# A two-layer Fourier-mixing and expert kernel on one core: row maxima by one reduction, buffers and order changed around them

## The chip, the cores and the metric

The kernel runs on one core of a Trainium2 chip, as one launch that takes the whole input and gives the whole output. The time is device microseconds of that core; the figure for the kernel is the median of its runs. The core has five engines that the text speaks of: TensorE (PE in the profile; its weight loads are listed as PEld), VectorE (DVE), ScalarE (ACT), GpSimd (POOL), and SyncE (SP), which issues the transfers. Each engine works through its own list of instructions in order; a semaphore holds an instruction back until what it reads is there and what it overwrites is free.

## The reference

The input x has 2048 tokens of width 512, in fp32. Two layers of two steps each follow, A and B twice with the same weights:

```python
def _A_ref(x, dft_seq_re, dft_seq_im, dft_hid_re, dft_hid_im):
    a = jnp.einsum("bsd,ed->bse", x, dft_hid_re)
    b = jnp.einsum("bsd,ed->bse", x, dft_hid_im)
    return jnp.einsum("ts,bse->bte", dft_seq_re, a) - jnp.einsum("ts,bse->bte", dft_seq_im, b)

def _B_ref(x, w_q, k1, k2, u, v):          # H = 32 heads, E = 16 keys per half, K = 2
    q = jnp.einsum("nd,dhc->nhc", xf, w_q)
    s1 = jnp.einsum("nhd,ed->nhe", q[..., :dk], k1)
    s2 = jnp.einsum("nhd,ed->nhe", q[..., dk:], k2)
    i1 = jnp.argsort(-s1, axis=-1)[..., :K]; i2 = jnp.argsort(-s2, axis=-1)[..., :K]
    ...                                     # 2 x 2 sums of the two best scores, the two best of these
    g = _softmax(top_s, axis=-1)
    act = _gelu(jnp.einsum("nd,nhkd->nhk", xf, u[top_e]))
    return jnp.einsum("nhk,nhk,nhkd->nd", g, act, v[top_e])

x = x + _A_ref(_layernorm(x), ...);  x = x + _B_ref(_layernorm(x), ...)   # twice
```

A is the real part of a Fourier transform along the tokens and along the width. B picks, for each token and each of 32 heads, two of 256 experts through two halves of 16 scores, and adds the experts' rows of v, weighted by softmax and gelu.

## The kernel before

Every fp32 matrix is kept as a high part, rounded to the format that PE reads at full rate, and a low part, the rest. A product is three matmuls: high with high, low with high, high with low. Names end in h and l for the parts (xh, xl; ch, cl; dh, dl; wh, wl; uh, ul; vh, vl; pth, ptl; ph, pl).

**Start.** The 16 tiles of 128 tokens of x are loaded (`wr`), and each is normalised: bn_stats (L245), bn_aggr (L254), the epsilon (L257) on VectorE, a power on POOL (L260), the product for the bias (L263) on VectorE, and then ACT writes xh (L271) and the normalised fp32, from which VectorE takes xl (L282, L287). Until the first of these is there, PE runs filler matmuls on the identity (L1135, 10 of them). Beside this the weights of B are prepared: query weights and keys are multiplied into wh and wl (L381 to L404), and dh, dl, uh, ul, vh, vl are split (L330).

**Transform along the tokens** (L434 on, matmuls at L518, for the first four tiles at L498). It runs in units of token tiles, in each of which all 16 tiles of x pass as weights under `piece`s of the matrix, loaded as `raw` and split into ch (ACT, L458) and cl (VectorE, L462). A unit of two tiles fills four accumulators; ACT and VectorE copy them out as pth and ptl (L543, L546).

**One token tile** (`token_tile`, L566): the transform along the width (L615), the addition to the row (L625), normalisation into `tok` (for the last tile in two halves, by ACT L271 and VectorE L649), transposition (L664); scores (L694, L698) that ACT copies to `sc` (L703); x times u (L725) and gelu (L730 to L745). VectorE then finds the two best of 16 per head and half. A tree of four maxima (`tree32`, L784 and three at L791, with the space `tmp`) gives the best value; a comparison with it (L778), a product with codes (L818) and a second tree in f16 (L800, L810) give its place; it is taken out of the scores (L827, L831), and the same again gives the second best. Gates follow (L854 to L894). Transposed (L903) and copied (`qt`, L907), the places make one-hot masks (`lr`: L926, weighted at L932); matmuls of masks (L943) give, per token, a 16 x 16 matrix of weights within blocks. ACT copies these blocks (`gs`, L955) into a buffer of the pool `sc`, and two transfers through memory (`gdr<-sc` at L999, `gt<-gdr` at L1006) bring the diagonal into rows. These weigh act (L1014), which is transposed (L1023), split into ph and pl (L1027, L1031) and multiplied with v (L1044, L1048); the sum goes to the row (L1064) and out (L1066).

The last tile of the program, 15, does all this in finer pieces: its maxima run in two halves of the heads (`halved`; 32 columns instead of 64), its masks live in the buffers of ch and cl, and matmuls with `picks` (L978) take the place of the transfers. While VectorE does its maxima, PE runs fillers (L1137).

**What sets the order.** Nothing is issued in the order in which it is written. A `Plan` collects all operations with a cost in microseconds, what they come after (`after`), what they only stand behind on the same engine (`behind`), the buffers they take and free, and a priority; `Plan.run` (L70 to L146) then builds each engine's list, always taking the operation that could start first, by priority among equals. The buffers' counts are in `BUFS` (`sc` 1, `lr` 4, `wr` 5, `c` 3). So a changed cost, buffer or dependence moves instructions of all engines from there on.

## Time and profile before

| | |
|---|---|
| median of 3 runs | 1266.33 us (1266.11 to 1267.36) |
| the profiled execution's own time | 1266.79 us |
| its span, first to last instruction | 1264.9 us |
| PE busy | 1250.8 us, 99% |
| VectorE busy | 994.2 us, 79% |
| ACT busy | 466.5 us, 37% |
| POOL busy | 45.7 us, 4% |
| transfers | 121.18 MB, 96 GB/s over the span |
| mean granted TensorE clock | 1.000 |

How to read it: matmuls are pipelined, so one lasts longer than the distance from its start to the next one's start, and PE counts as busy where only the distance matters. For PE the start-to-start distance is the price of a matmul. In a row of the timeline stand the start and the length in us, the engine, the line and the operation, output and inputs with shapes, how often, and in brackets the engine's idle time before it with what ended it. A row of groups ends with busy time and mean length in ns, and then the idle time before its instructions with what ended most of it. A row of waits has who waited for whom, the total in us, how often, and the longest.

### The profile page before, as it was taken

How to read it: one execution, taken by the hardware profiler on the slowest of the kernel's cores; microseconds unless marked ns; L12 is line 12 of the kernel's file. 1: busy time of each engine (PE TensorE's matmuls, PEld its weight loads, DVE VectorE, ACT ScalarE, POOL GpSimd, SP SyncE). 2: the span in 40 equal slices, each digit the busy share in tenths (PEclk: the TensorE clock that was granted, in tenths of full speed). 3: DMA queues.
4: the chain of work that ended last, by engine and by line, in shares of the span. 5: the costliest groups of instructions: out<-in, count | busy, mean ns of one | idle time of the engine just before them, and what ended most of it. 6: DMA issues, size and time to landing. Idle time of an engine off the chain costs nothing.

```text
span 1264.9 us, 20684 instructions
## 1 busy us (share of the span) xinstructions
PE 1250.8 (99%) x7804; PEld 1036.8 (82%) x7804; DVE 994.2 (79%) x2257; ACT 466.5 (37%) x966; POOL 45.7 (4%) x71
## 2 busy tenths in 40 slices
PE   9999999999999999999999999999999999999998
PEld 6777778887888888899878887888888888888886
DVE  8899998988887957779884378695685847778598
ACT  7522243343433333333563333333332433333232
POOL 2010000000000000000000000000000000000000
PEclk9999999999999999999999999999999999999999
DMA  7866541333233241413455204314142331414201
GB/s 235 268 197 213 180 150 34 92 70 65 67 84 76 76 101 50 112 39 88 121 133 135 67 26 104 81 59 109 42 108 51 93 91 51 108 43 110 58 9 35
DMA packets 224101, 121.18 MB, mean 96 GB/s; under 512 B 136448, under 2 KB 202496, under 8 KB 224000
## 3 DMA queue, kind: packets, MB, share of 16 engines
q1 hardware_dynamic: 224000, 119.85, 35.4%
q8 instruction: 61, 1.00, 0.3%
q14 instruction: 40, 0.33, 0.1%
HBM read 107.36 MB, written 12.45 MB: 95 GB/s over the span
## 4 chain that ended last, share of the span: by engine, by line
PE 71%; DVE 16%; issue 6%; DMA 2%; ACT 2%; SPq 1%; POOL 1%; POOLq 0%; DVEq 0%; ACTq 0%
PE acc L518 39%; PE bank L615 11%; PE bank L694 7%; PE bank L698 4%; PE bank L725 3%; DVE cl L462 2%; DVE w L384 2%; PE bank L1044 2%; DVE w L381 2%; PE bank L518 1%; PE bank L943 1%; DVE eq L778 1%; PE bank L1048 1%; PE bank L664 1%; POOL stats L260 1%
## 5 line engine op out<-in xcount | busy, mean ns | idle before, releaser
L518 PE MATMUL acc<-ch,xh 128*128 128x512 f32 (+1 forms) x1072 | 407.9, 381 | 0.0
L518 PE MATMUL acc<-ch,xl 128*128 128x512 f32 (+1 forms) x1072 | 397.8, 371 | 0.3 <-DVE xl L287 0.3
L518 PE MATMUL acc<-cl,xh 128*128 128x512 f32 (+1 forms) x1072 | 397.8, 371 | 0.0
L458 ACT CAST ch<-raw 128x512 fp32r<-128x512 f32 x256 | 158.4, 619 | 263.7 <-PE acc L518 227.0
L462 DVE TENSOR_TENSOR cl<-raw,ch 128x512 fp32r<-128x512 f32 x256 | 175.5, 687 | 72.4 <-ACT ch L458 52.9
L518 PEld LDWEIGHTS acc<-cl,xh 128*128 128x128 f32 x1072 | 201.9, 188 | 35.2
L518 PEld LDWEIGHTS acc<-ch,xh 128*128 128x128 f32 x1072 | 202.1, 189 | 32.6 <-issue 1.4
L518 PEld LDWEIGHTS acc<-ch,xl 128*128 128x128 f32 x1072 | 202.5, 189 | 31.6 <-DVE xl L287 1.0
L615 PE MATMUL bank<-dh,pth 128*128 128x512 f32 (+1 forms) x264 | 102.9, 392 | 0.4 <-ACT pth L543 0.4
L694 PE MATMUL bank<-wh,tok 128*128 128x512 f32 x256 | 100.2, 392 | 1.3 <-ACT sc L955 1.0
L615 PE MATMUL bank<-dl,pth 128*128 128x512 f32 (+1 forms) x264 | 100.6, 383 | 0.0
L694 PE MATMUL bank<-wl,tok 128*128 128x512 f32 x256 | 99.7, 390 | 0.0
L615 PE MATMUL bank<-dh,ptl 128*128 128x512 f32 (+1 forms) x264 | 95.9, 384 | 0.0
L784 DVE TENSOR_TENSOR tmp<-sc 128x512 f32<-128x512 f32 (+1 forms) x66 | 44.4, 672 | 61.7 <-ACT sc L703 60.8
L926 DVE TENSOR_TENSOR lr<-iota,qt 128x1024 f16<-128x1024 f16 x124 | 80.6, 684 | 10.6 <-ACT qt L907 10.6
L260 POOL TENSOR_TENSOR stats<-stats,half 128x1 f32<-128x1 f32 x64 | 44.4, 697 | 1183.7 <-DVE stats L257 1182.5
L778 DVE TENSOR_TENSOR eq<-sc,val 128x1024 f16<-128x1024 f32 (+1 forms) x66 | 78.5, 1190 | 1.5
L703 ACT COPY sc<-bank 128x512 f32<-128x512 f32 x64 | 36.8, 589 | 104.1 <-PE bank L698 73.1
L698 PE MATMUL bank<-wh,tok 128*128 128x512 f32 x256 | 68.5, 389 | 0.0
L800 DVE TENSOR_TENSOR eq<-eq 128x256 f16<-128x256 f16 (+3 forms) x198 | 60.0, 303 | 1.6
L615 PEld LDWEIGHTS bank<-dh,pth 128*128 128x128 f32 x264 | 49.6, 188 | 10.4 <-ACT pth L543 0.9
L694 PEld LDWEIGHTS bank<-wh,tok 128*128 128x128 f32 x256 | 48.1, 188 | 11.6 <-ACT raw L271 1.1
(152 smaller groups left out, 1790.7 us busy)
## 6 DMA issues: line engine op xcount, KB each, us to landing
raw<-in_cseq SPq DMA_DIRECT2D x224, 256.0 KB, 2.8
wr<-in_wq SPq DMA_DIRECT2D x32, 512.0 KB, 4.1
raw<-in_ctile SPq DMA_DIRECT2D x32, 256.0 KB, 2.9
wr<-in_x SPq DMA_DIRECT2D x16, 256.0 KB, 3.4
row<-in_x SPq DMA_DIRECT2D x16, 256.0 KB, 3.1
x2d<-row SPq DMA_DIRECT2D x16, 256.0 KB, 2.0
row<-x2d SPq DMA_DIRECT2D x16, 256.0 KB, 3.2
out<-row SPq DMA_DIRECT2D x16, 256.0 KB, 2.3
```

The source lines that it names most:

```text
L260: nc.gpsimd.tensor_tensor(st[:, 1:2], st[:, 1:2], half, op=ALU.pow)
L458: nc.scalar.copy(t[1], t[0])
L462: nc.vector.tensor_sub(t[2], t[0], as32(t[1]))
L518: nc.tensor.matmul(target(d), w[:, s, d * P:(d + 1) * P], moving(s % per, part), start=(s == 0 and k == 0 and d % blocks == 0), stop=(s == ...
L615: nc.tensor.matmul(t["y", cs.start], w[:, k, c, t0:t0 + P], r[:, c, k, cs], start=(z == 0 and c == 0 and m == 0), stop=(z == len(steps) - ...
L694: nc.tensor.matmul(t["pc", hf], t["th"][:, k, :], r[:, k, hf], start=(k == 0 and r is wh), stop=False)
L698: nc.tensor.matmul(t["pc", hf], t["tl"][:, k, :], wh[:, k, hf], start=False, stop=(k == KD - 1))
L725: nc.tensor.matmul(t["xu"], w[:, k, :], r[:, k, :], start=(m == 0), stop=(m == 3 * KD - 1))
L778: nc.vector.tensor_tensor(t["eq"][:, :, cols], flat("sc")[:, :, cols], val(rank_, cols), op=ALU.is_equal)
L784: nc.vector.tensor_max(t["tmp"][:, :, cols], flat("sc")[:, :8, cols], flat("sc")[:, 8:, cols])
L800: nc.vector.tensor_max(s[:, :m], s[:, :m], s[:, m:2 * m])
L926: nc.vector.tensor_tensor(t["m", hf, r], io2, row_of(r, hf), op=ALU.is_equal)
```

## The change

It has five parts.

1. `tree32` becomes one reduction (`largest`, new L826) over the innermost 16 elements. For that, the scores lie as (half, head, key) instead of (key, half, head): ACT copies a bank straight, the reduction reads 16 neighbours, and the two comparisons (new L820) and the subtraction (new L867) now read, and the latter writes, with a step of 16 elements, 64 bytes. `tmp` is gone. 66 trees of four operations become 66 reductions.
2. The masks' pool `lr` holds two buffers of both halves each instead of four of one half, and gs goes into the first of them when the matmuls have read it, instead of into the pool `sc`.
3. The transform along the width of a unit's second tile is planned behind that of its first.
4. `picks` lies ahead of uh and ul (160 bytes), a gap of 352 bytes stands ahead of vh and vl, and one of 128 bytes ahead of ph and pl. `half` becomes a column of `picks`.
5. The first tile of x is loaded and summed up in two halves; its xh is written by VectorE in two halves (new L316) right behind POOL; the matmuls of the first four tiles are grouped into high with high, low with high, and high with low, for tile 0 the first group in two parts; cl of piece 0 stands behind xh's halves and behind the epsilon of tile 1. One filler less stands at the start.

```diff
-            "tok": 3, "sc": 1, "eq": 1, "act": 3, "q": 2, "top": 1, "qt": 1, "lr": 4, "gt": 1, "pp": 1, "gdr": 2, "bn": 1}
+            "tok": 3, "sc": 1, "eq": 1, "act": 3, "q": 2, "top": 1, "qt": 1, "lr": 2, "gt": 1, "pp": 1, "gdr": 2, "bn": 1}
...
+    picks = const.tile([P, 40], F32, name="picks")
     uh = const.tile([P, KD, N], F32R, name="uh")
     ul = const.tile([P, KD, N], F32R, name="ul")
+    const.tile([P, 88], F32, name="gap")
...
-    half = const.tile([P, 1], F32, name="half")
-    picks = const.tile([P, P], F32, name="picks")
+    half = picks[:, 36:37]
...
+        mean = op("DVE", 0.1, f1, after, last=[h], prio=prio)
+        a = op("DVE", 0.1, f2, [mean], prio=prio)
+        xvar.setdefault(i, a)
         a = op("POOL", 0.5, f3, [a], prio=prio)
-        return op("DVE", 0.1, f4, [a], prio=prio)
+        return op("DVE", 0.1, f4, [a], prio=prio), a
...
+    def first_tile():
+
+        h, t, cut = Hold("wr"), {}, [slice(0, D // 2), slice(D // 2, D)]
+
+        def f_load(cs):
+            def f():
+                if not t:
+                    t[0] = setup_pool().tile([P, D], F32, name="wr", bufs=BUFS["wr"])
+                    t[1] = apool.tile([P, 2, 6], F32, name="bn", bufs=BUFS["bn"])
+                nc.sync.dma_start(t[0][:, cs], x_in[:P, cs])
+            return f
+
+        hb, stat = Hold("bn"), []
+        for z, cs in enumerate(cut):
+            a = xload[0] = op("SP", load(128), f_load(cs), take=[] if z else [h], prio=(-2, 0, 0, z), lag=2.3)
+            stat.append(op("DVE", dve(D // 2), lambda z=z, cs=cs: nc.vector.bn_stats(t[1][:, z], t[0][:, cs]), [a],
+                           take=[] if z else [hb], prio=(-3, 0)))
+        a, b = ln_rest(lambda: t[1].rearrange("p a b -> p (a b)"), hb, 0, stat, (-3, 0))
+        xhigh[0] = []
+        for cs in cut:
+            xhigh[0].append(op("DVE", 0.3, lambda cs=cs: nc.vector.tensor_scalar(
+                xh[:, 0, cs], t[0][:, cs], stats[:, 0, 0:1], stats[:, 0, 1:2], op0=ALU.subtract, op1=ALU.mult),
+                [b], prio=(-4, 0)))
+        a = op("ACT", act(512) + 0.18, lambda: ln_apply(t[0], t[0], 0), [a], behind=xhigh[0], prio=(-2, 0))
+        xready[0, 0] = op("DVE", dve(512), lambda: nc.vector.tensor_sub(xl[:, 0, :], t[0], as32(xh[:, 0, :])),
+                          [a], last=[h], prio=(-2, 0))
...
-            prio = (-2 if i < 8 else 0, i)
+            prio = (-5 if i == 1 else -2 if i < 8 else 0, i)
...
-            b1 = op("ACT", act(512), f1, [a], take=[hc], prio=(-1,) + turn)
-            c1 = op("DVE", dve(512), f2, [b1], last=[hr], prio=(-1,) + turn)
+            b1 = high[p] = op("ACT", act(512), f1, [a], take=[hc], prio=(-1,) + turn)
+            c1 = op("DVE", dve(512), f2, [b1], last=[hr], prio=(-1,) + turn,
+                    behind=xhigh[0] + [xvar[1]] if layer == 0 and at == 0 and p == 0 else [])
...
+                    def f(ds, w, part, s=s, moving=moving):
+                        def f():
+                            for d in ds:
+                                if s == 0 and w is xh and part == 0:
+                                    acc[d] = psum.tile([P, 2, T], F32, name=banks, bufs=BUFS[banks])
+                                nc.tensor.matmul(target(d), w[:, s, d * P:(d + 1) * P], moving(0, part),
+                                                 start=(s == 0 and w is xh and part == 0), stop=False,
+                                                 skip_group_check=True)
+                        return f
+
+                    halves_ = [range(KD // 2), range(KD // 2, KD)] if s == 0 else [range(KD)]
+                    for z, ds in enumerate(halves_):
+                        seq_last = op("PE", len(ds) * MM512, f(ds, xh, 0),
+                                      [high[s], xhigh[0][z] if s == 0 else xhigh[s], seq_last],
+                                      take=[hold[d] for d in ds] if s == 0 else [], prio=rank)
+                    seq_last = op("PE", KD * MM512, f(range(KD), xh, 1), [ready, seq_last], prio=rank)
+                    seq_last = xfree[s] = op("PE", KD * MM512, f(range(KD), xl, 0), [xready[layer, s], seq_last],
+                                             last=[hc], prio=rank)
...
-                       take=[hb] if z == 0 else [], behind=[a_row],
+                       take=[hb] if z == 0 else [],
+                       behind=[a_row] + ([hidden[n]] if n in hidden and at < len(units) - 1 else []),
                        last=[phold[layer, n]] if z == len(steps) - 1 else [], prio=prio)
+
+            hidden[n] = a
...
             def f_sc(hf=hf):
                 if hf == 0:
-                    t["sc"] = work([P, E, 2, H], F32, "sc")
-                nc.scalar.copy(t["sc"][:, :, hf, :], t["pc", hf].rearrange("p h e -> p e h"))
+                    t["sc"] = work([P, 2, H, E], F32, "sc")
+                nc.scalar.copy(t["sc"][:, hf], t["pc", hf])
...
-        def flat(name):
-            return t[name].rearrange("p e f h -> p e (f h)")
+        def flat():
+            return t["sc"].rearrange("p f h e -> p e (f h)")
...
-            def tree32(rank_, after):
-                def f0():
+            def largest(rank_, after):
+                def f():
                     new()
-                    nc.vector.tensor_max(t["tmp"][:, :, cols], flat("sc")[:, :8, cols], flat("sc")[:, 8:, cols])
-
-                a = [op("DVE", dve(8 * w), f0, after, take=[heq, hq, htop] if rank_ == 0 and z == 0 else [], prio=prio)]
-                for m in (4, 2, 1):
-                    def f(m=m):
-                        s = t["tmp"][:, :, cols]
-                        o = s[:, :m] if m > 1 else t["val"][:, rank_, cols][:, None, :]
-                        nc.vector.tensor_max(o, s[:, :m], s[:, m:2 * m])
-                    a = [op("DVE", dve(w * m), f, a, prio=prio)]
-                return a
+                    nc.vector.tensor_reduce(t["val"][:, rank_, cols], t["sc"].rearrange("p f h e -> p (f h) e")[:, cols],
+                                            axis=AX.X, op=ALU.max)
+
+                return [op("DVE", dve(16 * w), f, after, take=[heq, hq, htop] if rank_ == 0 and z == 0 else [], prio=prio)]
...
-            a = tree32(0, after)
+            a = largest(0, after)
...
             def f_off():
-                s = flat("sc")[:, :, cols]
+                s = flat()[:, :, cols]
...
-        made, hls = [], []
+        made, first_m, hls = [], [], [Hold("lr") for _ in range(2)] if not fine else []
+        spare_p = fine or layer and at == len(units) - 2 and i == tiles_of(n)[-1]
...
-                    t["m", hf, r] = piece((16, E, 4), ("ch", "cl")[r], F16) if fine else work([P, 16, E, 4], F16, "lr")
+                    if fine:
+                        t["m", hf, r] = piece((16, E, 4), ("ch", "cl")[r], F16)
+                    else:
+                        if hf == 0:
+                            t["mm", r] = work([P, 2, 16, E, 4], F16, "lr")
+                        t["m", hf, r] = t["mm", r][:, hf]
                     nc.vector.tensor_tensor(t["m", hf, r], io2, row_of(r, hf), op=ALU.is_equal)
 
-                hls.append(Hold("lr") if not fine else hls[-1] if r else Hold("c"))
-                a = op("DVE", dve(1024, 2), f_m, [a_qt], take=[] if fine and r else hls[-1:], prio=soon)
+                if fine:
+                    hls.append(hls[-1] if r else Hold("c"))
+                a = op("DVE", dve(1024, 2), f_m, [a_qt], take=([] if r else hls[-1:]) if fine else [] if hf else [hls[r]],
+                       behind=first_m[r:r + 1] if hf else [], prio=soon)
+                first_m.append(a)
...
-        spare_p = fine or soon != prio and i == tiles_of(n)[-1]
-        hgs, hbs = Hold("p" if spare_p else "sc"), [Hold("bank") for _ in range(2)]
+
+        hgs, hbs = Hold("p") if spare_p else hls[0], [Hold("bank") for _ in range(2)]
...
-                    t["gs"] = work([P, 16, 4, E], F32, "sc") if not spare_p else mixed().rearrange(
-                        "p (g t e) -> p g t e", t=4, e=E)
+                    m = mixed() if spare_p else t["mm", 0].rearrange("p f g e t -> p (f g e t)").bitcast(F32)
+                    t["gs"] = m.rearrange("p (g t e) -> p g t e", t=4, e=E)
...
+            if "ph" not in scopes:
+                scopes["ph"] = work_pool().tile([P, 32], F32, name="gap2", bufs=1)
```

The places in the order that the prediction speaks of. First VectorE at the start, before (here `wr` is a tile of x, `raw` a piece of the matrix; from its first statistics on):

```order
L245 BN_STATS bn<-wr 128x6
L254 BN_AGGR stats<-bn 128x2
L257 TENSOR_SCALAR stats<-stats 128x1
L462 TENSOR_TENSOR cl<-raw,ch 128x512
L263 SCALAR_TENSOR_TENSOR stats<-stats 128x1
L245 BN_STATS bn<-wr 128x6
```

and now:

```order
L311 BN_STATS bn<-wr 128x6 x2
L255 BN_AGGR stats<-bn 128x2
L258 TENSOR_SCALAR stats<-stats 128x1
L316 TENSOR_SCALAR xh<-wr,stats 128x256 x2
L246 BN_STATS bn<-wr 128x6
L264 SCALAR_TENSOR_TENSOR stats<-stats 128x1
L255 BN_AGGR stats<-bn 128x2
L258 TENSOR_SCALAR stats<-stats 128x1
L497 TENSOR_TENSOR cl<-raw,ch 128x512
```

cl of piece 0, which filled the time of POOL's power, stands behind the statistics of tile 1 and three small operations.

Second, VectorE some 45 us into the program, before:

```order
L330 TENSOR_TENSOR dl<-wr,dh 128x1024
L462 TENSOR_TENSOR cl<-raw,ch 128x512
L287 TENSOR_TENSOR xl<-wr,xh 128x512
L330 TENSOR_TENSOR dl<-wr,dh 128x1024
L462 TENSOR_TENSOR cl<-raw,ch 128x512
L287 TENSOR_TENSOR xl<-wr,xh 128x512
L332 SCALAR_TENSOR_TENSOR dl<-wr,dh 128x1024
```

and now:

```order
L365 TENSOR_TENSOR dl<-wr,dh 128x1024
L497 TENSOR_TENSOR cl<-raw,ch 128x512
L264 SCALAR_TENSOR_TENSOR stats<-stats 128x1
L291 TENSOR_TENSOR xl<-wr,xh 128x512
L497 TENSOR_TENSOR cl<-raw,ch 128x512
L291 TENSOR_TENSOR xl<-wr,xh 128x512
L365 TENSOR_TENSOR dl<-wr,dh 128x1024
```

The second dl stands behind both tiles' cl and xl.

Third, PE at the very end, from the last matmuls with picks. Before (ph and pl belong to tile 14, ch and cl are tile 15's parts of the same kind):

```order
L978 MATMUL bank<-picks,pth 64x16 x32
L1044 MATMUL bank<-vh,ph 128x512
L1044 MATMUL bank<-vl,ph 128x512
L1044 MATMUL bank<-vh,ph 128x512
L1044 MATMUL bank<-vl,ph 128x512
L1023 MATMUL bank<-identf,act 128x128 x2
L1048 MATMUL bank<-vh,pl 128x512 x2
L1044 MATMUL bank<-vh,ch 128x512
```

and now:

```order
L1023 MATMUL bank<-picks,pth 64x16 x32
L1068 MATMUL bank<-identf,act 128x128 x4
L1091 MATMUL bank<-vh,ph 128x512
L1091 MATMUL bank<-vl,ph 128x512
L1091 MATMUL bank<-vh,ph 128x512
L1091 MATMUL bank<-vl,ph 128x512
L1091 MATMUL bank<-vh,ch 128x512
```

Both tiles' transpositions (new L1068) stand ahead of all products with v, and tile 14's low part comes last. VectorE's last row additions (L1064, new L1111) of the two tiles stand together at the end of its list, and its pl (L1031) no longer stands among the masks of tile 15 (L926); a mask of tile 14 (new L968) stands ahead of the second half of tok of tile 15 (new L692).

39 lines of the change are left out of this document (14 added, 25 removed).

## The prediction

> **What bounds the kernel now.** I read the engine shares first, then busy time and granted clock by stretches of the program, and last the waits of PE.
>
> ```profile
> PE 1250.8 (99%) x7804; PEld 1036.8 (82%) x7804; DVE 994.2 (79%) x2257; ACT 466.5 (37%) x966; POOL 45.7 (4%) x71
> ...
> 0.00:46.00 46.00, 43.11 (x182) 33.34 (x182) 39.18 (x113) 35.31 (x53) 11.35 (x23) 1.00 0.76 240
> 46.00:200.00 154.00, 152.05 (x1332) 121.50 (x1332) 142.67 (x209) 45.27 (x93) 5.86 (x4) 1.00 0.59 187
> 200.00:400.00 200.00, 198.59 (x1169) 161.78 (x1169) 177.64 (x447) 74.34 (x168) 8.28 (x12) 1.00 0.30 71
> 400.00:640.00 240.00, 238.96 (x1505) 205.08 (x1504) 186.97 (x441) 94.61 (x199) 8.25 (x13) 1.00 0.34 84
> 640.00:900.00 260.00, 258.78 (x1465) 216.52 (x1464) 174.98 (x399) 94.61 (x192) 6.88 (x10) 1.00 0.34 86
> 900.00:1216.00 316.00, 316.00 (x1794) 263.82 (x1794) 231.46 (x531) 111.01 (x236) 4.52 (x8) 1.00 0.29 73
> 1216.00:1265.00 49.00, 43.32 (x372) 34.73 (x370) 41.29 (x121) 11.33 (x29) 0.56 (x1) 0.99 0.15 28
> ...
> PE bank L1023 <- DVE act L1014: 2.0, 4, 0.8
> PE bank L694 <- ACT sc L955: 1.0, 1, 1.0
> ```
>
> The windows give stretch, length, then busy time of PE, weight loads, DVE, ACT and POOL, and after them the granted clock. PE is the bound: its idle time is 2.9 us in the first 46, 2.0, 1.4, 1.0, 1.2 and 0.0 us in the five stretches of the body (5.6 together), and 5.7 us in the last 49, where most of its work is fillers besides. The clock is granted in full, so nothing is to be had there. PE's matmuls are the same before and after but for three fillers. So a gain can only come out of three places: the start, where PE waits for its first operand; the body's 5.6 us, of which the waits above are the largest single pieces; and the tail, which VectorE sets (41.3 busy of 49). VectorE's load in the body, 67 to 93% of a stretch, is worth nothing in itself.
>
> **The first tile.** Before, the chain is statistics, POOL's power, a product on VectorE, then ACT's xh. The timeline has start, duration, and in brackets the idle time before with what ended it; one row of the groups (busy us, mean ns) stands among them.
>
> ```profile
> 3.59 0.69 DVE L245 BATCH_NORM_STATS2 bn<-wr 128x6 f32<-128x512 f32 x1 [1.33 <-DMA wr<-in_x]
> ...
> 4.77 0.55 POOL L260 TENSOR_TENSOR stats<-stats,half 128x1 f32<-128x1 f32 x1 [2.88 <-DVE stats L257]
> ...
> 4.96 0.69 DVE L462 TENSOR_TENSOR cl<-raw,ch 128x512 fp32r<-128x512 f32 x1 [0.27 <-ACT ch L458]
> ...
> 6.22 0.69 DVE L245 BATCH_NORM_STATS2 bn<-wr 128x6 f32<-128x512 f32 x1 [0.50 <-DMA wr<-in_x]
> ...
> 6.62 0.50 PE L498 MATMUL acc<-ch,xh 128*128 128x512 f32 x1 [0.86 <-ACT xh L271]
> ...
> L649 DVE TENSOR_SCALAR tok<-row,stats 128x256 f32<-128x256 f32 x1 | 0.4, 411 | 0.0
> ...
> 45.29 0.39 PE L518 MATMUL acc<-ch,xl 128*128 128x512 f32 x1
> 45.52 0.39 PE L518 MATMUL acc<-cl,xh 128*128 128x512 f32 x1
> 45.74 0.39 PE L518 MATMUL acc<-ch,xh 128*128 128x512 f32 x1
> 46.45 0.50 PE L518 MATMUL acc<-ch,xl 128*128 128x512 f32 x1 [0.32 <-DVE xl L287]
> ```
>
> After, the statistics are taken in halves of the width, the first under the load of the second (I estimate 0.2 us won, out of 0.69 for the whole), and the two halves of xh are VectorE operations like L649 (0.41 each) right behind POOL, with L263 and ACT off the path. POOL then ends at 4.77 + 0.55 - 0.2 = 5.1, the first half is there at 5.5, and PE starts near 5.6, 1.0 us before 6.62. A matmul takes 0.225 us (45.29 to 45.74 is two). So the first four end at 6.5, and then PE needs cl of piece 0. VectorE's order puts cl behind the statistics of tile 1, which start only when that tile lands (6.22, with 0.50 us idle), and behind three small operations (from L245's end to POOL's start two of them and the handing over take 0.49; I take 0.35): 6.22 + 0.69 + 0.35 = 7.25, and cl is done at 7.95. Eight of tile 0's twelve matmuls remain and end near 9.8, against 6.62 + 12 x 0.225 = 9.3 before: +0.4. If tile 1 lands earlier, nothing waits and it is -0.9; its load stands behind one more issue now, which speaks against, and a load of two halves on other engines may end sooner, which speaks for it. Between the two I take -0.1.
>
> The order moves the two last tiles' cl and xl ahead of the second dl (1.2 us). The stall that the old order caused is in the last two rows: 45.74 to 46.45 is 0.71 for a matmul of 0.225, with xl late behind dl. **-0.5**, bounds -0.6 and 0. First 46 us: **-0.6** (-1.5 to +0.4).
>
> **One reduction for a tree.** Prices, from the groups kept apart by shape, and two neighbours in the tail for the pitch:
>
> ```profile
> L926 DVE TENSOR_TENSOR lr<-iota,qt 128x1024 f16<-128x1024 f16 x124 | 80.6, 684 | 10.6 <-ACT qt L907 10.6
> L778 DVE TENSOR_TENSOR eq<-sc,val 128x1024 f16<-128x1024 f32 x62 | 75.8, 1222 | 1.5
> ...
> L784 DVE TENSOR_TENSOR tmp<-sc 128x512 f32<-128x512 f32 x62 | 42.7, 689 | 61.6 <-ACT sc L703 60.8
> ...
> L791 DVE TENSOR_TENSOR tmp<-tmp 128x256 f32<-128x256 f32 x62 | 26.2, 422 | 1.3
> ...
> L791 DVE TENSOR_TENSOR tmp<-tmp 128x128 f32<-128x128 f32 x66 | 19.1, 289 | 1.6
> ...
> L397 DVE TENSOR_REDUCE ws<-bank 128x128 f32<-128x384 f32 x32 | 18.0, 561 | 0.0
> ...
> L791 DVE TENSOR_TENSOR val<-tmp 128x64 f32<-128x64 f32 x62 | 13.8, 223 | 1.6
> ...
> L778 DVE TENSOR_TENSOR eq<-sc,val 128x512 f16<-128x512 f32 x4 | 2.7, 687 | 0.0
> ...
> L784 DVE TENSOR_TENSOR tmp<-sc 128x256 f32<-128x256 f32 x4 | 1.7, 420 | 0.1
> ...
> L791 DVE TENSOR_TENSOR tmp<-tmp 128x64 f32<-128x64 f32 x4 | 0.9, 220 | 0.0
> ...
> L791 DVE TENSOR_TENSOR val<-tmp 128x32 f32<-128x32 f32 x4 | 0.8, 192 | 0.0
> ...
> 1239.53 0.69 DVE L778 TENSOR_TENSOR eq<-sc,val 128x512 f16<-128x512 f32 x1
> 1240.14 0.42 DVE L827 TENSOR_TENSOR eq<-iota,q 128x512 f16<-128x512 f16 x1
> ```
>
> A tree lasts 689 + 422 + 289 + 223 = 1623 ns. The reduction reads 1024 elements; L397, a reduction, reads 384 in 561 ns, and L778 reads 1024 in 1222, one row for the instruction's shape and one for its size: I take 1.22 us. That is 0.40 us less busy per tree, 62 times, 25 us of VectorE. Operations overlap: L778 lasts 0.69 and its follower starts after 0.61, so each costs about 0.08 less than it lasts; a full tree occupies 1.30 and a reduction 1.14.
>
> The new order of the scores makes both comparisons and the subtraction (L778 twice, L831 once per tile) step 64 bytes from element to element. Rows for it: L397 reads its bank at that step, and its 561 ns is what the line through L778's two sizes gives for 384 (1.045 ns per element, 687 - 128 x 1.045 = 553); L926 reads eight bytes of each 64 of iota in f16, 1024 elements in 684 ns. No row has a 64-byte step of fp32 in SBUF. Bounds: nothing, or half rate (another 1.07 us on a full operation, 1024 x 1.045 ns, 0.53 on a half one). I take nothing, as the nearest row is L397's.
>
> The Trainium skill speaks against the change here: "SBUF — State Buffer", section "Specifications (TRN2)", says that accesses have to hit a 16-byte line at least twice for full bandwidth, so every element at a 64-byte step would pay. By that rule rival D would be the case. No row of this trace tests it for fp32 in SBUF; L926's eight bytes per line are two hits at four bytes each and fit the rule too.
>
> In the body the shorter chain and the scores' buffer matter only where PE waits. ACT's waits on that buffer:
>
> ```profile
> ACT sc L955 <- DVE eq L778: 38.3, 15, 6.1
> ACT sc L703 <- DMA gdr<-sc: 14.0, 7, 3.2
> ```
>
> gs no longer needs the scores' buffer, so L955 loses its wait for the second comparison, and the next scores lose theirs for the diagonal's transfers. PE's wait of 1.0 us at L694 (on L955) should go, and some of the 2.0 at L1023. But every duration feeds the planner, so the whole body is laid out anew, and where a new wait comes up cannot be read from before. The body's idle 5.6 us is the most that can be won; the last stretch, with 0.0 in 316 us, shows that a layout may have none. I take **-1.0** (-4.5 to +3, the upper end as three waits of the longest kind above, 1.0 each).
>
> **The masks' buffer.** The first one is now held until the diagonal has gone out. Its next user is the following tile's first mask, tens of microseconds later; the most that this transfer ever held anybody is 3.2 us in the row above, and that on ACT. Nothing.
>
> **Second DFT tile by tile** only orders PE's own work: nothing by itself.
>
> **Offsets.** Matmuls with v differ from those of the sequence in one thing I can see, their time:
>
> ```profile
> L518 PE MATMUL acc<-ch,xl 128*128 128x512 f32 x880 | 343.5, 390 | 0.3 <-DVE xl L287 0.3
> L1044 PE MATMUL bank<-vl,ph 128*128 128x512 f32 x62 | 24.5, 395 | 0.0
> ```
>
> 5 ns more, on 186 matmuls: 0.9 us if the new offsets cure all of it, **-0.4** taken. For u (384 matmuls), no row says anything; 5 ns either way would be 1.9 us, nothing taken.
>
> **The tail.** Rows of its last 15 us:
>
> ```profile
> 1250.81 0.42 DVE L1031 TENSOR_TENSOR pl<-bank,ph 128x256 fp32r<-128x256 f32 x1
> ...
> 1258.78 0.20 PEld L1023 LDWEIGHTS bank<-identf,act 128*128 128x128 f32 x2 [0.40 <-DVE act L1012]
> ...
> 1259.68 0.19 PEld L1044 LDWEIGHTS bank<-vh,ch 128*128 128x128 f32 x1 [0.43 <-ACT ch L1027]
> ```
>
> Four trees of half width: 420 + 289 + 220 + 192 - 4 x 80 = 0.80 us each, a reduction 0.61; 4 x 0.19 = -0.77. The first tree has nothing to overlap with, so there some 0.2 more. pl (L1031, 0.42 - 0.08 = 0.33) leaves the row of masks, where it stood between two of them: -0.3. Against that, a mask of tile 14 (0.61, from L926) now stands before the second half of tok, which runs beside ACT's first half (0.6): +0.3. And tile 14's last row addition, which ran under matmuls, now stands with tile 15's behind them: +0.6 on VectorE, as L778's half for 512 elements. In return the matmuls there stand in another order, with tile 14's four ahead of where PE waited 0.43 for ch, and act's second product is no longer late (0.40): up to -0.8, I take -0.6. **-0.8** (-1.5 to +0.6).
>
> Sum: -0.6 - 1.0 - 0.4 - 0.8 = **-2.8 us**. The profiled execution ran 1266.79 us, span 1264.9, so its span would be 1262.1; it stands 0.46 above the median of the runs, 1266.33, so the median would be **1263.5**.
>
> **Rivals.** A (the sum), 1263.5, own range 1262 to 1265.
>
> B, more: cl of piece 0 is in time (-0.8 beyond A), and the body's new layout wins 3 instead of 1. 1260.7. For it: the body's last stretch shows no idle at all. Against: each wait there is a different one.
>
> C, no change: start at +0.4 with the stall at 45.7 kept (+1.0 against A), the body's waits only replaced (+1.0), offsets worth nothing (+0.4): 1265.9. For it: PE is busy 99%, and the trees' time in the body lay under PE's.
>
> D, slower, the stepped reads: comparisons and subtraction at half rate. The tail has six of them at half width; from 2.8 / 6 = 0.47 us extra on each they eat the whole sum, and half rate is 0.53, 3.2 in all: 1266.7 with the body unharmed. In the body a tile takes 3 x 1.07 = 3.2 us more and gets 2 x 0.16 back, while VectorE is 89% busy between 200 and 400: at some 33 us a tile (1016 us for 31 tiles) its load there would be 98%. If half of the 32 tiles hand 1 us on to PE, 1266.7 + 16 = **1283**. For it: no row reads fp32 so from SBUF. Against: L397 and, weakly, L926.
>
> E, slower, a worse layout: of the body's 32 tiles, eight get a new wait of 0.8 us as L1023 has now on L1014 (+6.4): 1269.9. For it: L1014 stands behind a round trip of transfers, and gs, masks and weights now share a buffer.
>
> **Chances.** A 0.45, B 0.22, C 0.20, D 0.07, E 0.06. What a measurement can tell from no change is 0.2%, 2.5 us: faster is below 1263.8, slower above 1268.9. A lies on both sides of the first, two thirds faster: 0.22 + 0.31 = 0.53 faster; 0.14 + 0.20 = 0.34 same; 0.13 slower. The range holds A, B with 1.4 us beyond it, and C and D's mildest form with 1.2 and 0.4: 1259.2 to 1267.0.
>
> **What would show it.** First real matmul near 5.6, then a gap before the cl matmuls (if none: B). No stall near 45.7. The reduction at 1.2 us for 128x1024, and comparisons still 1.22 (D if 2.3). No wait of ACT for the scores at the diagonal's transfer. Idle PE between 46 and 1216 near 4.6 us. Matmuls with v at 390. From the last DFT matmul to the last addition about 1 us less. I am wrong in the sum if the body's idle time moves by more than 2 us, or if PE's busy time does.

## The result: 5% slower

| | before | after |
|---|---|---|
| median, us | 1266.22 (1266.00 to 1267.36, 4 runs) | 1328.07 (1326.83 to 1328.94, 4 runs) |
| ratio, 95% interval | | 1.0486 (1.0468 to 1.0504) |
| span of the profiled execution, us | 1264.9 | 1325.1 |
| PE idle in the span, us | 14.1 | 60.0 |

62 us more, where 2.8 less were forecast. First the engine shares, the stretches (same columns as before: length, busy PE, weight loads, DVE, ACT, POOL, granted clock) and the largest waits of PE in the changed kernel:

```profile
PE 1265.1 (95%) x7801; PEld 1042.2 (79%) x7801; DVE 1042.5 (79%) x2062; ACT 464.2 (35%) x965; POOL 50.0 (4%) x71
...
0.00:46.00 46.00, 43.02 (x176) 32.52 (x177) 39.25 (x115) 33.25 (x50) 12.17 (x23) 1.00 0.77 239
46.00:200.00 154.00, 152.22 (x1335) 122.21 (x1334) 142.67 (x205) 45.91 (x94) 6.90 (x4) 1.00 0.60 187
200.00:400.00 200.00, 186.26 (x1105) 149.51 (x1104) 185.76 (x393) 72.00 (x166) 8.26 (x11) 1.00 0.28 67
400.00:640.00 240.00, 231.92 (x1423) 197.80 (x1422) 180.44 (x364) 82.62 (x174) 8.34 (x14) 1.00 0.30 75
640.00:900.00 260.00, 249.09 (x1447) 207.07 (x1446) 192.63 (x385) 99.17 (x201) 8.26 (x9) 0.99 0.33 87
900.00:1216.00 316.00, 305.65 (x1638) 249.85 (x1638) 223.45 (x434) 103.25 (x219) 4.39 (x8) 0.99 0.30 76
...
PE bank L939 <- DVE q L906: 24.1, 23, 2.7
PE bank L939 <- DVE q L928: 5.9, 13, 0.8
PE bank L1068 <- DVE act L1059: 5.7, 5, 2.1
```

Up to 200 us nothing has changed: the first tile's search for its maxima begins at 197.3 us. From there on PE is idle 8 to 14 us in every stretch. Half of its 60.0 us of idle time is one wait: at L939, the transposition of a tile's places and gates, PE waits for the last steps of VectorE's chain (L906, and L928 for the gates), 30.0 us in all. 24 of the 32 tiles wait there, for 0.3 to 2.7 us each. Some 13 us more are waits at L1068, the transposition of act, which VectorE also writes. VectorE itself is not full: 93% busy between 200 and 400, 71 to 75% later. Its groups of the search, kept apart by shape:

```profile
L820 DVE TENSOR_TENSOR eq<-sc,val 128x1024 f16<-128x1024 f32 x62 | 120.7, 1947 | 1.2
...
L826 DVE TENSOR_REDUCE val<-sc 128x64 f32<-128x1024 f32 x62 | 75.5, 1219 | 66.7 <-ACT sc L746 66.0
L867 DVE SCALAR_TENSOR_TENSOR sc<-eq,sc 128x1024 f32<-128x1024 f16 x31 | 63.2, 2038 | 0.6
```

The reduction lasts what was forecast, 1.22 us. The comparison went from 1222 to 1947 ns and the subtraction from 1223 to 2038: the step of 64 bytes is not free. Per tile that is 2 x 0.73 + 0.82 = 2.27 us more in the chain, against 2 x 0.16 that the reductions give back: about 1.95. The loss per tile is of that size on average: the span's 60.2 us more over 31 tiles are 1.94. It is not that in each tile, as eight of them do not wait at L939 at all. One tile, in the timeline of both engines:

```profile
678.51 2.05 DVE L867 SCALAR_TENSOR_TENSOR sc<-eq,sc 128x1024 f32<-128x1024 f16 x1
...
682.77 1.95 DVE L820 TENSOR_TENSOR eq<-sc,val 128x1024 f16<-128x1024 f32 x1
...
688.61 0.39 PE L557 MATMUL acc<-cl,xh 128*128 128x512 f32 x1
...
690.80 0.68 DVE L497 TENSOR_TENSOR cl<-raw,ch 128x512 fp32r<-128x512 f32 x1
691.40 0.22 DVE L906 TENSOR_TENSOR q<-key,df 128x128 f16<-128x128 f16 x1
...
691.68 0.34 PE L939 MATMUL bank<-ident,q 128*128 128x128 f16 x3 [2.68 <-DVE q L906]
691.83 0.56 PE L557 MATMUL acc<-ch,xh 128*128 128x512 f32 x1
692.18 0.63 PE L557 MATMUL acc<-ch,xl 128*128 128x512 f32 x1
```

PE has matmuls of the transform left (L557 goes on at once behind the transposes), but its list has the transposes first, and it stands still for 2.7 us. VectorE is never idle for long here; it is only later than the list assumed. Behind the wait the first matmuls last longer too (0.63 against 0.39): between 692.1 and 695.5 us the granted clock is 0.50. Three more such stretches of 3.4 us follow, from 1050.5, 1258.7 and 1316.7 us; at half clock each of the four costs about 1.7 us of PE's time (an estimate), together 7 of the 14 us by which PE's busy time grew (1250.8 to 1265.1).

### The profile page after: what moved, and what is told of

The parts are those of the page before. It is cut to its first block, busy times and chain, and to the rows that moved or that the text cites. A ratio compares the mean times of both kernels' runs of the same rounds, so it can differ in the third digit from the quotient of the medians.

```text
span 1325.1 us, 20456 instructions
## 1 busy us (share of the span) xinstructions
PE 1265.1 (95%) x7801; PEld 1042.2 (79%) x7801; DVE 1042.5 (79%) x2062; ACT 464.2 (35%) x965; POOL 50.0 (4%) x71
## 4 chain that ended last, share of the span: by engine, by line
PE 46%; DVE 42%; issue 5%; ACT 3%; DMA 3%; POOL 1%; SPq 0%; DVEq 0%; ACTq 0%
PE acc L557 21%; PE bank L655 10%; DVE eq L820 7%; DVE cl L497 5%; PE bank L737 4%; DVE sc L867 4%; DVE val L826 4%; DVE eq L836 3%; DVE eq L854 2%; DVE w L419 2%; DVE w L416 2%; PE bank L741 2%; DVE lr L968 2%; PE bank L1091 2%; PE bank L557 2%
## 5 line engine op out<-in xcount | busy, mean ns | idle before, releaser
L557 PE MATMUL acc<-ch,xh 128*128 128x512 f32 (+1 forms) x1072 | 411.4, 384 | 0.1
L557 PE MATMUL acc<-cl,xh 128*128 128x512 f32 (+1 forms) x1072 | 399.7, 373 | 0.7 <-DVE cl L497 0.7
L557 PE MATMUL acc<-ch,xl 128*128 128x512 f32 (+1 forms) x1072 | 399.5, 373 | 0.4 <-DVE xl L291 0.3
L557 PEld LDWEIGHTS acc<-cl,xh 128*128 128x128 f32 x1072 | 203.4, 190 | 37.1 <-DVE cl L497 1.1
L557 PEld LDWEIGHTS acc<-ch,xh 128*128 128x128 f32 x1072 | 203.7, 190 | 32.5 <-ACT xh L290 0.5
L557 PEld LDWEIGHTS acc<-ch,xl 128*128 128x128 f32 x1072 | 203.8, 190 | 31.7 <-DVE xl L291 1.1
L826 DVE TENSOR_REDUCE val<-sc 128x64 f32<-128x1024 f32 (+1 forms) x66 | 78.3, 1186 | 67.1 <-ACT sc L746 66.4
L820 DVE TENSOR_TENSOR eq<-sc,val 128x1024 f16<-128x1024 f32 (+1 forms) x66 | 124.9, 1892 | 1.2
L261 POOL TENSOR_TENSOR stats<-stats,picks 128x1 f32<-128x1 f32 x64 | 48.7, 763 | 1236.7 <-DVE stats L258 1236.7
L968 DVE TENSOR_TENSOR lr<-iota,qt 128x1024 f16<-128x1024 f16 x124 | 80.7, 683 | 1.8 <-ACT qt L943 1.8
L585 DVE TENSOR_TENSOR ptl<-acc,pth 128x512 fp32r<-128x512 f32 x62 | 42.8, 691 | 30.3 <-ACT pth L582 30.1
L867 DVE SCALAR_TENSOR_TENSOR sc<-eq,sc 128x1024 f32<-128x1024 f16 (+1 forms) x33 | 65.3, 1980 | 0.6
```

The costliest lines, as they stand in the source:

```text
L261: nc.gpsimd.tensor_tensor(st[:, 1:2], st[:, 1:2], half, op=ALU.pow)
L557: nc.tensor.matmul(target(d), w[:, s, d * P:(d + 1) * P], moving(s % per, part), start=(s == 0 and k == 0 and d % blocks == 0), stop=(s == ...
L820: nc.vector.tensor_tensor(t["eq"][:, :, cols], flat()[:, :, cols], val(rank_, cols), op=ALU.is_equal)
L826: nc.vector.tensor_reduce(t["val"][:, rank_, cols], t["sc"].rearrange("p f h e -> p (f h) e")[:, cols], axis=AX.X, op=ALU.max)
L867: nc.vector.scalar_tensor_tensor(s, t["eq"][:, :, cols], -BIG, s, op0=ALU.mult, op1=ALU.add)
L968: nc.vector.tensor_tensor(t["m", hf, r], io2, row_of(r, hf), op=ALU.is_equal)
```

## The experiments

Theory 1: the stepped reads make VectorE's chain late, and PE's fixed list turns that into waits. Theory 2: it is the rest of the change (masks' buffer, order, offsets, start). All ratios are to the kernel before on the same chip.

| run | median us | ratio (95%) |
|---|---|---|
| e1 straight reads, same order | 1260.58 | 0.9968 (0.9957 to 0.9980) |
| e2 plan told the real costs | 1269.49 | 1.0039 (1.0025 to 1.0053) |
| e3 parts 2 to 5, with the tree | 1262.41 | 0.9978 (0.9969 to 0.9986) |
| e4 part 1 alone | 1334.21 | 1.0540 (1.0524 to 1.0556) |
| e5 search kept as (head, key) | 1278.23 | 1.0110 (1.0095 to 1.0125) |
| e7 part 4 alone | 1279.42 | 1.0118 (1.0101 to 1.0135) |
| e8 part 5 alone | 1300.62 | 1.0288 (1.0272 to 1.0303) |
| e9 scores in pairs of heads | 1261.90 | 0.9972 (0.9962 to 0.9982) |
| e10 part 4, phase kept | 1264.32 | 0.9994 (0.9985 to 1.0003) |
| e11 part 5, phase kept | 1284.86 | 1.0154 (1.0140 to 1.0167) |
| e12 part 2 alone | 1272.31 | 1.0057 (1.0044 to 1.0070) |
| e13 before, plan told too little | 1293.34 | 1.0219 (1.0204 to 1.0234) |
| e14 as e11, one number of the plan | 1279.71 | 1.0111 (1.0096 to 1.0126) |
| e15 as e3, one number of the plan | 1262.46 | 0.9977 (0.9968 to 0.9987) |
| e16 as before, one number of the plan | 1272.13 | 1.0048 (1.0031 to 1.0065) |

**The steps taken away, the order kept (e1).**

```diff
-        def flat():
-            return t["sc"].rearrange("p f h e -> p e (f h)")
+        def flat(cols):
+            s = t["sc"][:, cols.start // H:cols.stop // H].rearrange("p f h e -> p (f h e)")
+            return s.rearrange("p (e x) -> p e x", e=E)
```

> The changed kernel with the same instructions in the same order on every engine; only the two comparisons and the subtraction read (and the subtraction writes) the scores straight through instead of with a step of 64 bytes, so the wrong scores are compared: it leaves out the right pairing of score and maximum, and its output is not the reference's. Theory 1 (the stepped reads, 0.73 us more per comparison and 0.82 per subtraction, are what delays every tile): L820 back at 1.22 us, L867 at 1.22, and the kernel at 1263 (1260 to 1267). Theory 2 (the masks' buffer, the order of the second transform or the new layout of the whole program delays PE, the steps being beside it): stays above 1300. A mixture: in between.

Measured: 1260.58. Its groups:

```profile
L821 DVE TENSOR_TENSOR eq<-sc,val 128x1024 f16<-128x1024 f32 x62 | 75.7, 1221 | 1.2
...
L868 DVE SCALAR_TENSOR_TENSOR sc<-eq,sc 128x1024 f32<-128x1024 f16 x31 | 37.9, 1222 | 0.6
```

Same instructions, same order, same buffers: the whole 67 us between this run and the change come from the step of these three operations. Theory 2 falls for the change as a whole.

**Part 1 alone (e4)** in the kernel before, and **all but part 1 (e3)**, with `tree32`, `tmp` and the old layout of the scores put back in the changed kernel:

> The kernel before with part 1 alone: scores as (half, head, key), one reduction, stepped comparisons and subtraction, all else as before. Theory 1: slow by itself, 1310 to 1340. Theory 2: within 5 us of 1266.

> Parts 2 to 5 of the change alone: scores as before and the tree of four maxima in place of the reduction, with its space. Theory 1: the parts that the stepping does not touch are worth what was forecast for them, start, body, offsets and a tail without the trees: 1264.3 (1261 to 1267). Theory 2: above 1300.

1334.21 and 1262.41: part 1 is slow by itself, and the other four together are worth 2.8 us (ratio 0.9978).

**The plan told the truth (e2), or a lie (e13).** Is VectorE's added work the loss, or its being unknown to the plan?

```diff
-codes([op("DVE", dve(16 * w), eq(0), a, prio=prio)])
+codes([op("DVE", dve(16 * w * 1.69), eq(0), a, prio=prio)])
```

and the same for eq(1), with 1.77 for f_off. In e13 the kernel before has these costs divided by the same numbers, and no operation is changed.

> The changed kernel whole, but the plan is told what the stepped operations take (1.69 times the elements for a comparison, 1.77 for the subtraction). Theory 1a (PE's fixed list puts the transposes of a tile's places where the plan believes them done, some 2 us too early for each of 30 tiles; VectorE has the time): most of it comes back, 1266 to 1285. Theory 1b (VectorE is full, its work is what delays): 1305 or more.

> The kernel before, no operation changed; only the plan is told that comparisons and subtraction cost 1/1.69 and 1/1.77 of what they do, so it errs by the same ratio as in the change, without the 48 us of added work on VectorE. Theory 1a (the error of the plan is enough): the error is 0.44 to 0.46 us on each of three operations per tile, 1.4 against 2.2 to 2.3 in the change, so 20 to 40 us are lost: 1285 to 1305, with PE waiting for the places' transposes (L903). Theory 1b (VectorE's added work is needed for the loss): below 1272.

e2 has the slow operations whole (VectorE busy 1037 us) and takes 1269.49: 59 of the 67 us between the change and e1 come back by the order alone. PE's row for the transposes in e2:

```profile
L939 PE MATMUL bank<-ident,q 128*128 128x128 f16 x96 | 11.1, 225 | 0.0
```

No idle time stands before it, where the change had 30.0 us. And e13 loses 28 us with no operation slowed. PE's idle time grows from 14.1 to 29.7 us, and more than half of the growth is in the place that theory 1a names:

```profile
PE bank L903 <- DVE q L870: 9.4, 13, 1.3
```

So the plan's error is enough to lose, and VectorE's work has room when the plan knows of it. 9 us are left between e2 and e1. From the last matmul of the transform along the width to the end, e2 takes 38.4 us and e1 36.5, so 2 of the 9 are the tail's; PE's idle time between 46 and 1216 us is 5.5 against 1.8 (1.9 us of it at L557 for xl, 1.5 at L988), so some 4 are waits. Whether they are the price of the work itself is not shown, as another plan of the same operations can differ by as much (e16 below).

**What a step costs (e6).** The comparison of rank 0, of rank 1, the subtraction and the second reduction get four other patterns:

```diff
+nc.vector.tensor_tensor(..., s.rearrange("p (r k j) -> p k r j", k=8, j=2), ...)      # pairs, 64 bytes apart
+nc.vector.tensor_tensor(..., s.rearrange("p (a r j) -> p j a r", j=4, a=2), ...)      # singles, 16 bytes apart
+nc.vector.scalar_tensor_tensor(s, ...)          # s: "p (r j) -> p j r", j=8: singles, 32 bytes apart
+nc.vector.tensor_reduce(...)                    # s: "p (e x) -> p x e": 256 bytes apart, 31 of 62
```

> The changed kernel in its own order, with other steps in four of its operations for the 62 full ones; it computes nothing useful: the first comparison reads pairs (8 bytes) at a step of 64 bytes, the second single elements at a step of 16 bytes, the subtraction reads and writes single elements at a step of 32 bytes, the second reduction reads at a step of 256 bytes. If a 16-byte line has to be used twice for full speed: pairs 1.22 us, singles at 16 bytes 1.95 (as at 64), subtraction at 32 bytes 2.04, second reduction 1.95. If it is the distance that costs: pairs above 1.22, singles at 16 bytes near 1.22.

It ran once, in 1338.82 us, and only the lengths of its operations are read here:

```profile
L842 DVE TENSOR_REDUCE val<-sc 128x64 f32<-128x1024 f32 x62 | 99.4, 1603 | 67.3 <-ACT sc L746 66.6
...
L885 DVE SCALAR_TENSOR_TENSOR sc<-eq,sc 128x1024 f32<-128x1024 f16 x31 | 67.9, 2191 | 0.6
L831 DVE TENSOR_TENSOR eq<-sc,identf 128x1024 f16<-128x1024 f32 x31 | 61.4, 1981 | 0.0
...
L826 DVE TENSOR_TENSOR eq<-sc,identf 128x1024 f16<-128x1024 f32 x31 | 37.7, 1216 | 0.0
```

Pairs at 64 bytes are free (L826, 1216 ns); singles cost 1981 ns already at 16 bytes (L831), no more at 64 (1947). L842 is the mean of 31 straight reductions (1219) and 31 at 256 bytes, which makes the latter 2 x 1603 - 1219 = 1987. The Trainium skill's rule in "SBUF — State Buffer", section "Specifications (TRN2)", two accesses to a 16-byte line for full bandwidth, agrees with these rows. The price of a miss, for which the section has no figure, is 1.6 times the straight time here for a read, and 1.7 to 1.8 times for the subtraction, which also writes so.

**A layout without slow steps (e9, e5).** e9 lays the scores out by these rows, two neighbours together:

```diff
-                    t["sc"] = work([P, 2, H, E], F32, "sc")
-                nc.scalar.copy(t["sc"][:, hf], t["pc", hf])
+                    t["sc"] = work([P, 2, H // 2, E, 2], F32, "sc")
+                nc.scalar.copy(t["sc"][:, hf], t["pc", hf].rearrange("p (x j) e -> p x e j", j=2))
```

> The whole change with the scores as (half, pair of heads, key, head of the pair): the reduction steps by 8 bytes, two elements to a 16-byte line, and the comparisons read pairs of 8 bytes; the one-hot for the subtraction is made in the same order by two operations of half size, so that the subtraction runs straight. By the prices run (pairs at full speed, singles not) nothing steps slowly: reduction, comparisons and subtraction at 1.22 us, the kernel at 1260.6 plus at most 0.5 for the added operations (1260 to 1262), faster than both kernels. If it is the distance after all, comparisons are slow and it is above 1265.

```profile
L832 DVE TENSOR_TENSOR eq<-sc,val 128x1024 f16<-128x1024 f32 x62 | 75.8, 1223 | 1.2
L838 DVE TENSOR_REDUCE val<-sc 128x64 f32<-128x1024 f32 x62 | 75.4, 1217 | 57.5 <-ACT sc L749 56.8
...
L883 DVE SCALAR_TENSOR_TENSOR sc<-eq,sc 128x1024 f32<-128x1024 f16 x31 | 37.9, 1223 | 0.6
```

All at full speed, with the whole computation in place: 1261.90, faster than both kernels (0.9972). The reduction reads single elements here, but 8 bytes apart, two in 16 bytes, and lasts 1217 ns as when straight. Against e3, the tree, the run gains 0.5 us, less than the intervals tell apart. So one reduction is worth nothing to speak of here, even where it costs nothing.

e5 instead keeps the whole search as (head, key), with runs of 16 keys:

> The changed kernel with the whole search kept as (head, key): comparison, codes, f16 tree, one-hot and subtraction all run straight over 16 neighbouring keys per head, so that nothing steps by 64 bytes in fp32; plan and order as in the change. Theory 1: the straight fp32 operations take 1.22 us and the kernel 1260.6 as in the run with straight reads, if the f16 operations keep their 0.68 us with runs of 16, 8, 4 and 2 neighbours and with a value held over 16 elements. If these fall to one element per step (1.22), VectorE loses up to 2 us a tile against the plan and the kernel ends up as slow as the change itself, 1300 or more. I lean to the first, 1260 to 1266.

```profile
L860 DVE TENSOR_TENSOR eq<-gap,q 128x1024 f16<-128x1024 f16 x31 | 38.0, 1225 | 0.9
...
L843 DVE TENSOR_TENSOR q<-eq 128x128 f16<-128x128 f16 x31 | 12.6, 407 | 0.6
```

The fp32 operations are at 1.22, but the f16 one-hot against a value held over 16 elements falls from 692 to 1225 ns and the last step of the tree from 221 to 407. Again the plan does not know it: 1278.23. It is the miss that I had named and thought less likely, at a smaller price: the time lies in neither of the two ranges.

**Offsets (e7, e10).** Part 4 alone; e10 adds `const.tile([P, 8], F32, name="pad")`.

> The kernel before with part 4 alone, the offsets; the order is that of before. Both theories: matmuls with v at 390 ns instead of 395, 186 of them, 0.9 us; with u perhaps 0 to 0.8. 1264.9 for a before of 1266.3, a ratio of 0.999.

> Part 4 alone as in the run before it, but with 32 bytes of padding, so that the pieces of the matrix, tok and pth stay where they were (128 beyond a multiple of 512, like xh, dh and wh) instead of moving to 96. Theory of the phase (a matmul of 512 columns takes 4 ns longer when its two operands start at different places within 512 bytes, which the moved buffers caused): L518 back at 390, products with v at 390 instead of 395, 1264 (0.9 to 1.7 below before). If the 15 us came from elsewhere in part 4: near 1279 again.

e7, then e10:

```profile
L519 PE MATMUL acc<-ch,xl 128*128 128x512 f32 x880 | 347.9, 395 | 0.0
```

```profile
L520 PE MATMUL acc<-ch,xl 128*128 128x512 f32 x880 | 343.2, 390 | 0.0
...
L1048 PE MATMUL bank<-vl,ph 128*128 128x512 f32 x62 | 24.2, 391 | 0.0
```

Both theories had e7 near 1264.9; it missed. Without part 5's larger bn, the removal of half moves every later buffer by 32 bytes: in the program's addresses ch and cl start at 96 instead of 128 beyond a multiple of 512, while xh, dh and wh stay at 128. All matmuls of the transforms and scores with 512 columns then last 395 ns, and the products with v stay at 395 (ph at 96, vh at 128). PE's busy time is 1268.1 us in e7, 17 more than before, and the kernel is slower by 15. With the padding they are at 390, and so are the products with v: that is the cure the prediction counted, 186 x 5 ns = 0.9, and the run is at 0.9994, which a measurement cannot tell from 1.

**Start, masks, and the plan's own scatter (e8, e11, e12, e14 to e16).** e8 is part 5 alone, e11 the same with half moved into picks so that no buffer moves, e12 part 2 alone. e14, e15 and e16 are e11, e3 and the kernel before with one number changed:

```diff
-MM512, MM256, TR32, TR16, MMG = 0.2275, 0.1203, 0.12, 0.057, 0.0156
+MM512, MM256, TR32, TR16, MMG = 0.2280, 0.1203, 0.12, 0.057, 0.0156
```

> The kernel before with part 5 alone, the first tile by halves. Theory 1 (the parts are worth their terms of the sum): the first matmul at 5.5, a wait of 0.5 for cl, the stall of 0.5 near 45.7 gone or moved, -0.6 in all (ratio 0.9995), with the rest laid out anew by up to 2 us either way. Theory 2 would have the start slower.

> Part 5 alone, with half moved into picks so that the larger bn does not push the pieces, tok and pth from 128 to 160: by the theory of the phase the 36 us of the first run of this part are the moved buffers' (18 us of matmul time, and a plan that no longer fits it), and 1265.5 (1263 to 1268) is left. If the first tile itself or its order were slow: above 1280.

> Part 2 alone, the masks' two double buffers with gs in the first. Theory 1: ACT's waits for the scores' buffer go (38 and 14 us in all), PE's few waits with them: 1264.5 (1263 to 1267). Theory 2 (the buffer held until the diagonal has gone out delays the next masks): above 1270.

> Part 5 alone with the phase kept, and the plan told that a matmul of 512 columns costs 0.2280 instead of 0.2275 us; nothing else. Theory of the layout (the 13 us between 262 and 287, where PE had ten matmuls of the transform per kind fewer to fall back on, are an accident of this one plan): the hole moves or goes, 1262 to 1278. If part 5 itself costs it: 1283 to 1287 again.

> Parts 2 to 5 with the tree, the plan told 0.2280 for 0.2275. If layouts scatter by accident: anywhere from 1262 to 1280, so that 1262.4 was partly a good layout. If not: 1262 to 1263.5.

> The kernel before, the plan told 0.2280 for 0.2275. As for the run of parts 2 to 5: 1265 to 1285 if layouts scatter, 1265 to 1267 if not.

The phase explains 16 of e8's 36 us; 20 are left in e11, and I had expected none. Its stretch, a part of it and, within 262 to 287 us, two groups of PE:

```profile
200.00:400.00 200.00, 186.37 (x1062) 152.10 (x1061) 168.94 (x422) 68.91 (x159) 7.00 (x10) 0.95 0.28 66
...
270.00:290.50 20.50, 12.59 (x75) 8.85 (x75) 11.22 (x30) 8.26 (x22) 1.09 (x2) 0.50 0.55 90
...
L1082 PE MATMUL bank<-vh,ph 128*128 128x512 f32 x4 | 2.8, 711 | 2.7 <-ACT ph L1065 2.7
...
L556 PE MATMUL acc<-cl,xh 128*128 128x512 f32 x4 | 1.6, 389 | 0.0
```

There PE has 10 matmuls of the transform (4 of the kind shown) where the kernel before had 42, so that it follows one tile's chain from wait to wait, 13 us idle. From 270.0 to 290.5 us the granted clock is 0.50, and a product with v, 395 ns elsewhere, lasts 711. With one number of the plan changed by 0.2% (e14) the stretch has 195.2 us busy and the kernel is 5 us faster, between the two ranges that were expected for it. The kernel before, with the same number changed, is 6.6 us slower by the medians (e16), and no operation differs. e3 stays where it is (e15).

So a part made alone is judged with whatever plan it gets. The traces show where: from the last matmul of the transform along the width to the end, before takes 37.2 us and e11 37.4, but e16 46.6 and e14 46.7. e12 is one of these too. It reaches that matmul 3.3 us earlier than before (1224.4 against 1227.7) and then takes 47.5 us, where e3, which holds part 2 as well, takes 37.4. In these tails the weighing of tile 13's act (called tile 14 ahead of the prediction; by the kernel's order of units it is 13) stands near the end and waits for its transfers; e12, then e16:

```profile
1264.83 0.43 DVE L1023 TENSOR_TENSOR act<-act,raw 128x256 f32<-128x256 f32 x1 [4.57 <-DMA raw<-gdr]
```

```profile
1264.98 0.43 DVE L1014 TENSOR_TENSOR act<-act,raw 128x256 f32<-128x256 f32 x1 [1.55 <-DMA raw<-gdr]
```

So e12's 1272, which its second theory had (above 1270), is no sign of that theory: no mask waits for its buffer there, and the order alone can do as much. Part 5 costs 19.5 us with the old number (e11) and 7.6 with the new one (e14 against e16). What parts 2 and 5 are worth by themselves stays open; only their sum with 3 and 4 is measured, e3.

## Why the prediction was wrong

**What bounds** was right: PE, and of VectorE only what PE waits for.

**The step that failed** is "I take nothing, as the nearest row is L397's". The bounds were nothing and half rate, 1.07 us; measured were 0.73 for a comparison and 0.82 for a subtraction. L397 reads a bank, not SBUF, and so was no row for it; L926, the other one, reads 8 bytes in a line, which e6 shows to be free just where single elements are not. The rows fitted both theories, and I took the one that left the sum as it was. The Trainium skill's rule, weighed beside them ("SBUF — State Buffer", section "Specifications (TRN2)"), spoke against the change, and e6 agrees with it. In the sum the body was to win 1.0 us, at worst to lose 3; PE's idle time between 46 and 1216 us went from 5.6 to 44.9.

**Rival D** had the mechanism, a chance of 0.07, and the wrong price, 1283. It reckoned with VectorE's load near 98% and half of the tiles handing 1 us on. VectorE was at 93%, and the loss is 1.9 us a tile on average, because the place at which PE waits is fixed by the plan's costs: a chain that is late makes PE late, however idle VectorE is elsewhere (e2, e13). It is no fixed price per tile: in e13 an error of 1.4 us a tile lost 0.9. The sentence "VectorE's load in the body is worth nothing in itself" was right and should have led there.

**The other terms**, which e1 and e3 measure without the step:

- First tile. The timeline of the change:

```profile
4.97 0.73 DVE L316 TENSOR_SCALAR xh<-wr,stats 128x256 fp32r<-128x256 f32 x2 [0.67 <-POOL stats L261]
5.75 0.69 DVE L246 BATCH_NORM_STATS2 bn<-wr 128x6 f32<-128x512 f32 x1
...
6.79 0.69 DVE L497 TENSOR_TENSOR cl<-raw,ch 128x512 fp32r<-128x512 f32 x1
...
5.53 1.49 PE L534 MATMUL acc<-ch,xh 128*128 128x512 f32 x4
7.54 1.19 PE L534 MATMUL acc<-cl,xh 128*128 128x512 f32 x4 [0.52 <-DVE cl L497]
...
9.47 1.07 PE L534 MATMUL acc<-ch,xh 128*128 128x512 f32 x4
```

  The first matmul at 5.53 (forecast 5.6), then the wait for cl. Tile 1 had landed by 5.75 and nothing waited for it, so cl began at 6.79, not 7.25, and tile 1's first matmul starts at 9.47. Before, it starts at 9.48 (the 9.3 of the prediction was reckoned, not read): nothing won, for -0.1 taken.
- The stall at 45.7: gone there, but PE waits 0.3 us for xl at 32.8 in the change and in e3, and at 33.0 in e11, as long as it did before 46.45. PE's busy time of the first 46 us did not move (43.1, 43.0). -0.5 was wrong: it moved.
- Body: PE idle between 46 and 1216 is 2.3 us in e3 and 1.8 in e1, for 5.6 before: -3.3 and -3.8 for -1.0 taken. This was rival B's size. ACT's waits for the scores' buffer on the transfers are gone as forecast, and no mask waits for its buffer in either run.
- Offsets: 395 to 390 ns, all of the 0.9 us where 0.4 was taken.
- Tail: from the start of the last matmul of the transform along the width to the end it is 37.2 us before, 36.5 in e1 and 37.4 in e3, where the tree is still there: -0.8, as forecast, all of it the reductions'.

Together e1 runs at 1260.6, 4.7 us below the kernel before on its chip, where rival B had 5.6 below; e9, which pairs scores and maxima as they belong, is 3.4 below.

**Rival E**, a worse layout, had a chance of 0.06 and eight waits of 0.8. The runs e11, e12 and e16 show layouts 7 to 20 us apart; for this change it did not happen (e1), but its size was too small.

## What to carry to other kernels

Before a layout is turned for one operation's sake, go through all other readers of the buffer and count how many bytes of each 16 they use in a row; look for a row that reads the same memory with the same width, and where there is none, measure it or put the bound into the forecast. In a kernel whose order is built from costs, an operation's true length matters twice, and the second time more: here 65 to 70 us more work (VectorE busy 1037 and 1042 us against 972 in e1), on an engine idle for 230 us and more, cost 9 us when the plan knew of it and 67 when it did not. A part of a change tried alone changes the plan and the addresses too; compare it with the plan held, or with several plans.

## What was not expected of the hardware

- fp32 in SBUF, single elements at steps of 16, 64 and 256 bytes: 1.95 to 1.99 us for 1024, against 1.22 straight, in pairs (e6) or at 8 bytes (e9's reduction); reading and writing at 64 and 32 bytes, 2.04 and 2.19.
- f16 on VectorE: against a value held over 16 neighbours 1225 ns for 1024 elements (692 with the value varying); held over pairs, as in e9, two operations of 512 at 420 ns each.
- Matmuls of 512 columns last 390 ns (a start every 227 ns) when both operands begin at the same place within 512 bytes, and 395 (a start every 233) when one is 32 bytes off (e7, e8): 15 us of this kernel for a shift of 32 bytes. Whether 512 bytes or a smaller step is what counts, no run tells.
- Where PE had 13 us of idle time within 25, the granted clock was 0.50 for 20.5 us, and a matmul lasted 711 instead of 395 ns (e11). One wait of 2.7 us in the change was followed by 3.4 us at 0.50.
